# Plain stores of a gated FNet and feed-forward kernel issued by SyncE in place of GpSimd

## The chip, the cores and the metric

The kernel runs on one core of one Trainium2 chip. The metric is the device time of one launch in microseconds (us). Before the change it is 1788.1 us, the median of three runs (1788.05 to 1788.41).

## The reference, cut to what matters

```python
g = sigmoid((x * gate_w).sum(-1, keepdims=True))
a = einsum("bsd,ed->bse", x, dft_hid_re)
b = einsum("bsd,ed->bse", x, dft_hid_im)
y = einsum("ts,bse->bte", dft_seq_re, a) - einsum("ts,bse->bte", dft_seq_im, b)
h = relu(einsum("bsd,df->bsf", x, w1) + b1) ** 2
out = einsum("bsf,fd->bsd", h, w2) + b2
return g * y + (1 - g) * out
```

x is 2048 x 1024, w1 is 1024 x 3584, w2 is 3584 x 1024, the two sequence matrices are 2048 x 2048 and the two hidden ones 1024 x 1024, all in float32.

## The kernel before, in words

There are five matrix products: x (the two DFTs along the hidden dimension), a and b (the two parts of x times w1), c (the DFT along the sequence) and o (h times w2). Each is done by a scheme of Strassen and Winograd in seven products of halves, numbered 1 to 7, and most of these are split once more in the same way. So operands are sums of blocks (S1 to S4 on the left, T1 to T4 on the right). Each operand is then split in a high and a low part, rounded to the type of fast float32: ScalarE writes the high one (L203, L407), VectorE the low one (L211, L415, L418). Three matmuls (high by high, low by high, high by low) make one product of blocks. All matmuls are issued at one place (L1425). Results leave PSUM by ScalarE or VectorE (L308, L321, L329), and a group of matmuls that continues an older sum has it copied into PSUM first by ScalarE (L255).

The kernel's text holds its own planner. It first lists all operations (`Op`) and all steps of TensorE. From the fixed order of the steps it works out a due time for each operation, and then it goes backward from those to a planned start (L1134 to L1150), with SLACK (L89) held back, 3 us for SyncE and 2 us for GpSimd, and with SOON (L88), the time within which a result that is to be evicted should leave. Then it simulates the run forward. In this it has 55 slots in SBUF for blocks of 512 KB, two DMA rings (`rings`, L1182), one that SyncE and one that GpSimd feeds, which share 390 GB/s (L24, `rate`, L1185), and costs such as n/960 + 0.064 us for n elements on VectorE (L152). `try_engine` (L1326) lets each engine begin the first operation by planned start that is ready at the simulated moment, at most 15 us ahead (AHEAD, L67). GUARD (L87) holds back other work when the eviction of a PSUM group is about to be ready: within the first number of us, operations with a planned start later than the eviction's by more than the second number wait. The order in which the simulation begins operations is the order of the instructions on each engine of the chip, where semaphores alone time them. The order of the matmuls doesn't depend on the simulation.

Transfers: `load` (L164, issued at L166) and `back` (L445) are issued by SyncE. GpSimd issues three kinds. `accumulate` (L169, issued at L172) reads a block from DRAM and adds it to a block in SBUF, and `add_to` (L476) and the adding of o's part to the output (L976) are alike. Plain stores are `store` (L175, issued at L177) and `out` of the class Seven (L435, issued at L438). `store` writes what later stages read: `ab` and `h` (results of x, and of a and b), `out` (the gated part of c), `e` (sums made early, EARLY, L83) and `t` (sums that go to DRAM when made and are loaded again in a later product: THROUGH_X, THROUGH_C and THROUGH_O, L95 to L99). All `t` are blocks that an accumulating transfer has just made. `out` writes spilled results (`v`). A plain store of the gate vector of 8 KB (L901) has a line of its own. On each engine's queue instructions start in order: one that waits for a semaphore holds up those behind it.

`EARLY` gives sums that are made ahead of the stage that uses them: for b_l a store is due at 75 us and then every 15 us, four of them. The opening (`prologue`, L1438) and the last group (`by_row`, L979) have instructions of their own.

Of the kernel before, what the change touches and what calls it, by code (L numbers as in the profile page):

```python
# [16 lines left out]
P = 128  # L17
# [12 lines left out]
         5), ("a", 3), ("x", 3), ("b", 3), ("a", 7), ("x", 7), ("b", 7), ("x", 4), ("a", 4), ("b", 4), ("c", 0), ("o",  # L30
         0))
ORDER_C = (1, 2, 5, 6, 3, 7, 4)
ORDER_O = (1, 2, 5, 6, 3, 7, 4)
# [30 lines left out]
BY_DMA = {"x_l": ("S1", "S2", "S3", "S4"), "x_r": ("T1", "T4"), "h_l": ("S4",), "c_l": ("S1", "S2", "S3", "S4"),  # L64
          "c_r": ("T1", "T2", "T3", "T4"), "o_l": ("S3", "S4"), "o_r": ("T2", "T3", "T4")}
# [13 lines left out]
CHAIN = {"c": {1: 1, 2: 1, 3: 1, 4: 1, 5: 2, 6: 1, 7: 1}, "o": {3: 1, 1: 1, 2: 1, 4: 1, 6: 1, 7: 1, 5: 1}}  # L79
# [3 lines left out]
EARLY = {"a_l": (("S2", "S1"), (), 70.0, 7.5), "b_l": (("S2",), (), 75.0, 15.0), "x_r": (("T1",), (), 40.0, 7.5)}  # L83
# [3 lines left out]
GUARD = (0.7, 3.0)  # L87
SOON = {"POOL": 12.0, "ACT": 6.0, "DVE": 6.0}  # L88
SLACK = {"SP": 3.0, "POOL": 2.0, "ACT": 0.6, "DVE": 0.6}  # L89
LEAD = {"SP": 3.0, "POOL": 1.0, "ACT": 2.0, "DVE": 2.0}  # L90
GATE = (320.0, 5.0)
# [6 lines left out]
THROUGH_C = ("T2",)  # L98
THROUGH_O = ("T2",)  # L99
# [3 lines left out]
def gated_mix_kernel(ctx: ExitStack, tc: tile.TileContext, x4, xn, w4, ct, w1a, w1b, w2, b1, b2, gw, out):  # L103
# [15 lines left out]
    class Val:  # L119
# [6 lines left out]
        def ap(self):  # L126
            return self.tile[:, :, :self.width]
# [293 lines left out]

    class Seven:
# [25 lines left out]
        def keep(self, name, vs):  # L448

            far = [i for i, runs in enumerate(SPILL.get(name, ())) if self.name and self.name in runs]  # L450
            self.have[name] = vs
            there = None
            if far:
                place = self.place if name == "s" and self.name in ADD_S else None
                there = {k: self.out(v, k, place and Far(place(k).at)) for k, v in vs.items()}
            self.kept[name] = far, there, [0]

        def get(self, name):
            far, there, n = self.kept[name]
            n[0] += 1  # L460
            if n[0] - 1 in far:
                vs = {}
                for k, f in there.items():
                    vs[k] = self.back(f, k)
                    if name == "s":
                        mark = ops[-1].also = Fixed()
                        ops[-1].then = lambda t, mark=mark: setattr(mark, "ready", t)
                        self.marks.append((k, mark))
                return vs
            return self.have[name]  # L470
# [8 lines left out]
        def do(self, p):  # L479
            get, product, place = self.get, self.product, self.order.index  # L480
            first, second = (5, 7) if place(5) < place(7) else (7, 5)
            summed = self.name and self.name in SUMMED
            mid = {5: ((0, 1), 3), 7: ((1, 0), 4)}
            if p == 1:
                self.keep("one", (yield from product(1, None, None)))
            elif p == 2:
                yield from product(2, get("one"), (0, 0))
            elif p == 6:
                self.keep("u", (yield from product(6, get("one"), None)))
            elif summed and p == first:  # L490
                self.keep("s", (yield from product(p, get("u"), None)))
            elif summed and p == second:
                t = yield from product(p, None, None)
                far_s, far_u = self.name in ADD_S and self.place, self.name in ADD_U
                s, u, w = None if far_s else get("s"), self.kept["u"][1] if far_u else get("u"), {}
                assert not far_s or place(mid[first][1]) < place(second)
                for k in self.keys:
                    if far_s:
                        dst, f = self.place(k), self.kept["s"][1][k]
                        Op("POOL", 0.6, 2 * P * 4 * 512 * 2, [t[k], f] + [m for j, m in self.marks if j == k], dst,  # L500
                           lambda k=k, dst=dst: nc.gpsimd.dma_start(dst.at, t[k].ap(), accum_op=ADD)).twice = True
                    else:
                        self.final((1, 1), k, both(s[k], t[k], self.rows, k[-1]))
                    w[k] = self.add_to(t[k], k, u[k]) if far_u else both(u[k], t[k], self.rows, k[-1])
# [112 lines left out]
    def tall(name, left, right, ksteps, order, second, less, final, from_ps, by_row=None):  # L617
# [4 lines left out]
        def product(p, old, quad):  # L622
# [23 lines left out]
            l2 = {q: Inner(lambda m, j, q=q: View(base[j, q], 256 * m), INNER_L, 256) for q in range(k2)}  # L646
# [45 lines left out]
            def twice(q, p2):  # L692
                again[q].made.update({key: r2[q].of(key) for key in ("T1", "T2")})
                l_, r_ = FACTORS[p2]
                step(operand(l2[q].of(l_), p in less), operand(again[q].of(r_)), groups[p2])
# [33 lines left out]
        run = Seven(order, 4, keys, product, final)  # L729
        for p in order:  # L730
            for _ in run.do(p):
                pass

# [44 lines left out]
    def x_stage():  # L778
# [17 lines left out]
        left.update({(m, q): Side(x_block(m, q), PLUS_L, BY_DMA["x_l"],  # L796
# [3 lines left out]
        right = {(q, c): Side(lambda j, n, q=q, c=c: Far(w4[n, c, j, q], 0.0), MIX_R, BY_DMA["x_r"], through=THROUGH_W,  # L800
# [11 lines left out]
    def h_stage(part):  # L812
# [38 lines left out]
        left = {(m, q): Side(lambda i, j, m=m, q=q: Far(w1[i, m, j, q], 0.0), MIX_L, BY_DMA["h_l"], rows * P,  # L851
# [66 lines left out]
    def c_stage():  # L918
# [21 lines left out]
        left = {q: Side(lambda i, j, q=q: ab[j, q, i], PLUS_L, BY_DMA["c_l"], through=THROUGH_C,  # L940
                        made={f: c_forms[f, q] for f in C_FORMS}) for q in range(8)}
        right = {(q, c): Side(lambda j, n, q=q, c=c: Far(ct[n, c, j, q], 0.0), PLUS_R, BY_DMA["c_r"], through=THROUGH_C, made=had("c_r", (q, c)))
                 for q in range(8) for c in range(2)}
        tall("c", left, right, 8, ORDER_C, TWICE_C, LESS_C, lambda quad, k, v: end(quad, k, v, lambda: v.tile),
# [11 lines left out]
    def o_stage():  # L956
# [37 lines left out]

        left = {q: Side(lambda i, j, q=q: Far(w2[i, j, q], 0.0), MIX_L, BY_DMA["o_l"], through=THROUGH_O, made=had("o_l", q)) for q in range(7)}
        right = {(q, c): Side(lambda j, n, q=q, c=c: h_far[j, q, 2 * n + c], PLUS_R, BY_DMA["o_r"], through=THROUGH_O,
                             made={f: o_forms[f, q, c] for f in O_FORMS})
                 for q in range(7) for c in range(2)}
        tall("o", left, right, 7, ORDER_O, TWICE_O, LESS_O, lambda quad, k, v: end(quad, k, v, lambda: v.tile),
# [36 lines left out]
    def had(side, at):  # L1036
        return {f: early[side, at, f] for f in EARLY.get(side, ((),))[0]}

# [3 lines left out]
    runs = {"x": x_stage(), "a": h_stage(0), "b": h_stage(1)}  # L1042
    for name, p in ORDER:
        a, b = len(ops), len(steps)
        if name in ("c", "o"):
            (c_stage if name == "c" else o_stage)()
        else:
            parts = [runs[r].do(ALIKE[p] if r == "x" and TOGETHER else p) for r in name]
            while parts:
                parts = [g for g in parts if next(g, done) is not done]  # L1050
        marks.append((f"{name}{p}", a, len(ops), b, len(steps)))
# [507 lines left out]
```

## Time and profile before

| what | us |
|---|---|
| median of three runs | 1788.1 |
| the profiled execution | 1788.53 |
| its span, from the first to the last instruction | 1786.7 |
| TensorE busy | 1780.1 |
| VectorE busy | 1637.1 |
| ScalarE busy | 1027.1 |
| GpSimd busy | 296.6 |

The profiled execution is 1.83 us longer than its span and 0.43 us longer than the median. Busy time doesn't count the issuing of DMAs on SyncE. On GpSimd the issuing instruction itself is shown as busy.

### The profile page before, as it was taken

How to read it: one execution, taken by the hardware profiler on the slowest of the kernel's cores; microseconds unless marked ns; L12 is line 12 of the kernel's file. 1: busy time of each engine (PE TensorE's matmuls, PEld its weight loads, DVE VectorE, ACT ScalarE, POOL GpSimd, SP SyncE). 2: the span in 40 equal slices, each digit the busy share in tenths (PEclk: the TensorE clock that was granted, in tenths of full speed). 3: DMA queues.
4: the chain of work that ended last, by engine and by line, in shares of the span. 5: the costliest groups of instructions: out<-in, count | busy, mean ns of one | idle time of the engine just before them, and what ended most of it. 6: DMA issues, size and time to landing. Idle time of an engine off the chain costs nothing.

```text
span 1786.7 us, 21834 instructions
## 1 busy us (share of the span) xinstructions
PE 1780.1 (100%) x7868; PEld 1473.8 (82%) x7868; DVE 1637.1 (92%) x1696; ACT 1027.1 (57%) x1224; POOL 296.6 (17%) x422
## 2 busy tenths in 40 slices
PE   9999999999999999999999999999999999999998
PEld 8888888888888888888888888888888888888887
DVE  8886999999799897999998999659999998999998
ACT  7444744324669576876574737436576434673753
POOL 0102211011211322101133202212000022211120
PEclk9999999999999999999999999999999999999999
DMA  9919989988969999789899959999675996997993
GB/s 378 387 56 291 286 296 309 362 323 265 291 249 370 311 283 334 259 291 308 234 241 269 240 175 318 303 274 268 233 258 191 375 274 184 313 315 169 299 269 73
DMA packets 144237, 488.03 MB, mean 273 GB/s; under 512 B 15728, under 2 KB 29376, under 8 KB 144128
## 3 DMA queue, kind: packets, MB, share of 16 engines
q0 software_dynamic: 58928, 210.27, 45.8%
q1 hardware_dynamic: 84496, 275.17, 42.0%
q8 instruction: 62, 1.02, 0.2%
q10 hardware_dynamic: 704, 1.18, 0.2%
q14 instruction: 47, 0.39, 0.1%
HBM read 376.98 MB, written 109.58 MB: 272 GB/s over the span
## 4 chain that ended last, share of the span: by engine, by line
PE 99%; ACT 1%; DMA 0%; DVE 0%; issue 0%
PE ps L1425 99%; DMA raw<-in_x 0%; ACT hi L203 0%; ACT ps L255 0%; DVE o L960 0%; DVE o L989 0%; ACT both L407 0%; ACT acc L308 0%; ACT hi L1464 0%; ACT both L203 0%
## 5 line engine op out<-in xcount | busy, mean ns | idle before, releaser
L1425 PE MATMUL ps<-hi,both 128*128 128x512 f32 x2072 | 640.8, 389 | 0.3 <-ACT ps L255 0.3
L1425 PE MATMUL ps<-hi 128*128 128x512 f32 x1574 | 611.3, 389 | 0.5 <-ACT hi L1464 0.5
L1425 PE MATMUL ps<-lo,hi 128*128 128x512 f32 x1574 | 611.2, 389 | 0.0
L1425 PE MATMUL ps<-hi,lo 128*128 128x512 f32 x1574 | 611.2, 389 | 0.0
L1425 PEld LDWEIGHTS ps<-hi,both 128*128 128x128 f32 x2072 | 389.1, 188 | 82.0 <-ACT ps L255 1.4
L203 ACT ACTIVATE hi<-raw 128x1024 fp32r<-128x1024 f32 (+1 forms) x315 | 321.7, 1037 | 217.0 <-DVE raw L182 82.9
L1425 PE MATMUL ps<-lo,both 128*128 128x512 f32 x1036 | 403.3, 389 | 0.0
L211 DVE TENSOR_TENSOR lo<-raw,hi 128x1024 fp32r<-128x1024 f32 (+1 forms) x279 | 337.0, 1218 | 43.6 <-ACT hi L203 39.0
L1425 PEld LDWEIGHTS ps<-hi 128*128 128x128 f32 x1574 | 295.5, 188 | 62.0 <-ACT hi L1464 0.8
L1425 PEld LDWEIGHTS ps<-lo,hi 128*128 128x128 f32 x1574 | 295.5, 188 | 61.3
L1425 PEld LDWEIGHTS ps<-hi,lo 128*128 128x128 f32 x1574 | 295.6, 188 | 61.2
L203 ACT ACTIVATE hi<-sum 128x1024 fp32r<-128x1024 f32 (+1 forms) x230 | 234.5, 1030 | 182.3 <-DVE sum L182 123.5
L211 DVE TENSOR_TENSOR lo<-sum,hi 128x1024 fp32r<-128x1024 f32 (+1 forms) x195 | 235.2, 1211 | 6.2 <-ACT hi L203 3.7
L1425 PEld LDWEIGHTS ps<-lo,both 128*128 128x128 f32 x1036 | 194.5, 188 | 40.2
L308 ACT ACTIVATE acc<-ps 128x1024 f32<-128x1024 f32 (+1 forms) x142 | 139.5, 987 | 123.9 <-PE ps L1425 118.8
L321 DVE TENSOR_TENSOR acc<-acc,ps 128x1024 f32<-128x1024 f32 (+1 forms) x152 | 172.5, 1140 | 39.9 <-PE ps L1425 38.1
L182 DVE TENSOR_TENSOR raw<-raw 128x1024 f32<-128x1024 f32 (+1 forms) x131 | 152.0, 1178 | 0.1
L203 ACT ACTIVATE both<-sum 128x512 fp32r<-128x512 f32 x148 | 92.2, 625 | 101.3 <-DVE sum L388 57.3
L255 ACT ACTIVATE ps<-acc 128x1024 f32<-128x1024 f32 (+1 forms) x83 | 81.2, 980 | 69.4 <-DVE acc L321 54.1
L321 DVE TENSOR_TENSOR back<-back,ps 128x1024 f32<-128x1024 f32 x64 | 71.9, 1129 | 14.8 <-PE ps L1425 14.3
L407 ACT ACTIVATE both<-raw 128x512 fp32r<-128x512 f32 x111 | 68.4, 619 | 27.6 <-PE ps L1425 16.7
L182 DVE TENSOR_TENSOR sum<-raw,sum 128x1024 f32<-128x1024 f32 (+1 forms) x65 | 77.8, 1197 | 1.0 <-PE ps L1425 0.9
(69 smaller groups left out, 1193.3 us busy)
## 6 DMA issues: line engine op xcount, KB each, us to landing
raw<-h SPq DMA_DIRECT2D x92, 512.0 KB, 6.5
raw<-in_ct SPq DMA_DIRECT2D x91, 512.0 KB, 7.6
raw<-in_w SPq DMA_DIRECT2D x81, 512.0 KB, 7.5
back<-v SPq DMA_DIRECT2D x48, 512.0 KB, 6.5
raw<-in_ct POOLq DMA_DIRECT2D x48, 512.0 KB, 12.7
raw<-ab SPq DMA_DIRECT2D x40, 512.0 KB, 13.7
t<-raw POOLq DMA_DIRECT2D x38, 512.0 KB, 12.4
sum<-t SPq DMA_DIRECT2D x38, 512.0 KB, 18.3
```

The lines of the kernel that those rows point to most:

```text
L182: Op("DVE", c, l, [a, b], w, lambda: nc.vector.tensor_tensor(w.ap(), a.ap(), b.ap(), op=op), over=[a, b])
L203: nc.scalar.activation(self.hi()[:, k, :], src(v)[:, k, :], AF.Copy, scale=-1.0 if less else 1.0)
L211: nc.vector.tensor_tensor(a, b, c, op=SUB)
L255: lambda rp=rp, k=k, e=e, v=v: nc.scalar.activation(self.ps[rp][:, :k, :], v.tile[:, e:e + k, :], AF.Copy),
L308: group.take(seg, rp, Op("ACT", c, l, [], w, lambda: nc.scalar.activation(view(w.tile, rows, rp), view(group.ps[rp], rows, rp), AF.Copy, s ...
L321: nc.vector.tensor_tensor(a, b, d, op=ADD)
L407: Op("ACT", c, l, [v.base], hi, lambda: nc.scalar.activation(self.hi(), cols(v), AF.Copy, scale=-1.0 if less else 1.0), then=lambda t: set ...
L1425: nc.tensor.matmul(group.ps[r // group.per][:, r % group.per, :], a()[:, kk, r * P:(r + 1) * P], b()[:, kk, :], start=first and kk + n == ...
```

## The change

All calls of `store` and of `out` are issued by SyncE, at a planned cost of 0.06 us in place of 0.6, and the planner counts them to SyncE's ring. GpSimd keeps the accumulating transfers and the store of the gate vector at L901. Five numbers of the planner change (EARLY for b_l, GUARD, SOON for GpSimd, which now also serves SyncE, GATE by 0.8 us, CHAIN for product 7 of c), and in stage o the sum S1 of left block 0 goes through DRAM. The remaining edits restate tables or add paths that this setting doesn't take: BY_DMA and THROUGH_C as counts of blocks (8 is all of them), c and o in the same list of the order as the rest and in the same order as before, and `Lefts`, which with MERGE empty makes the operands that `Inner` made. CHAIN for product 7 of c isn't used, as that product isn't split again.

```diff
-ORDER_C = (1, 2, 5, 6, 3, 7, 4)
-ORDER_O = (1, 2, 5, 6, 3, 7, 4)
...
-CHAIN = {"c": {1: 1, 2: 1, 3: 1, 4: 1, 5: 2, 6: 1, 7: 1}, "o": {3: 1, 1: 1, 2: 1, 4: 1, 6: 1, 7: 1, 5: 1}}
+CHAIN = {"c": {1: 1, 2: 1, 3: 1, 4: 1, 5: 2, 6: 1, 7: 2}, "o": {3: 1, 1: 1, 2: 1, 4: 1, 6: 1, 7: 1, 5: 1}}
...
-EARLY = {"a_l": (("S2", "S1"), (), 70.0, 7.5), "b_l": (("S2",), (), 75.0, 15.0), "x_r": (("T1",), (), 40.0, 7.5)}
+EARLY = {"a_l": (("S2", "S1"), (), 70.0, 7.5), "b_l": (("S2",), (), 68.7, 11.9), "x_r": (("T1",), (), 40.0, 7.5)}
+MERGE = ""
+STORES = "SP"
...
-GUARD = (0.7, 3.0)
-SOON = {"POOL": 12.0, "ACT": 6.0, "DVE": 6.0}
+GUARD = (1.2, 8.0)
+SOON = {"POOL": 18.0, "ACT": 6.0, "DVE": 6.0}
...
-GATE = (320.0, 5.0)
+GATE = (320.8, 5.0)
...
-THROUGH_C = ("T2",)
-THROUGH_O = ("T2",)
+THROUGH_C = {"T2": 8}
+THROUGH_O = {"T2": 8, "S1": 1}
...
     def store(dst, v, ap=None):
-        Op("POOL", 0.6, 2 * P * 4 * v.width * 2 / 2, [v], dst,
-           lambda: nc.gpsimd.dma_start(dst.at, v.ap() if ap is None else ap(v.tile)))
+        q, c = (nc.sync, 0.06) if STORES == "SP" else (nc.gpsimd, 0.6)
+        Op(STORES, c, 2 * P * 4 * v.width * 2 / 2, [v], dst,
+           lambda: q.dma_start(dst.at, v.ap() if ap is None else ap(v.tile))).soon = True
...
+        def of(self, key):
...
+            return operand(self.plain.of(key), self.less)
...
         def out(self, v, k, f=None):
 
             f, n = f or far(f"v{len(ops)}"), min(2, self.rows - 2 * k[-1])
-            Op("POOL", 0.6, P * 4 * 512 * n, [v], f, lambda: nc.gpsimd.dma_start(f.at[:, :n, :], v.tile[:, :n, :]))
+            q, c = (nc.sync, 0.06) if STORES == "SP" else (nc.gpsimd, 0.6)
+            Op(STORES, c, P * 4 * 512 * n, [v], f, lambda: q.dma_start(f.at[:, :n, :], v.tile[:, :n, :])).soon = True
             return f
...
-                step(operand(l2[q].of(l_), p in less), operand(r2[q].of(r_)), groups[p2])
+                step(l2[q].of(l_), operand(r2[q].of(r_)), groups[p2])
...
-            o.due = min(o.due, (made or at[o.step]) + SOON[o.eng])
+            o.due = min(o.due, (made or at[o.step]) + SOON.get(o.eng, SOON["POOL"]))
```

## Rows read from the trace of the kernel before

**Rows 1.** The page: span, busy time and share of each engine.

```profile
span 1786.7 us, 21834 instructions
...
PE 1780.1 (100%) x7868; PEld 1473.8 (82%) x7868; DVE 1637.1 (92%) x1696; ACT 1027.1 (57%) x1224; POOL 296.6 (17%) x422
```

**Rows 2.** The chain that ended last, in order of time: start, length, what.

```profile
5.79 1669.49 PE ps L1425 x7362
...
1682.64 1.02 ACT ps L255
...
1683.70 96.91 PE ps L1425 x426
...
1782.81 0.69 DVE o L989
```

**Rows 3.** Waits of TensorE's weight loads: us in total, times, longest.

```profile
PEld ps L1425 <- ACT ps L255: 1.4, 3, 0.7
```

**Rows 4.** Timeline of TensorE's matmuls: start, us, engine, line, operation.

```profile
1660.37 0.39 PE L1425 MATMUL ps<-lo,both 128*128 128x512 f32 x1
...
1678.73 0.39 PE L1425 MATMUL ps<-lo,both 128*128 128x512 f32 x1
...
1781.57 0.39 PE L1425 MATMUL ps<-hi,both 128*128 128x512 f32 x1
```

**Rows 5.** Plain stores on GpSimd, L177: ns min/median/max, first and last start.

```profile
L177 POOL DMA_DIRECT2D t<-raw x38: 532/552/1519, 152.3 to 1531.4; - x38
...
L177 POOL DMA_DIRECT2D h<-h x12: 532/534/563, 177.5 to 740.8; - x12
```

**Rows 6.** The same of the spills, L438.

```profile
L438 POOL DMA_DIRECT2D v<-acc x28: 532/534/580, 236.8 to 421.1; - x28
L438 POOL DMA_DIRECT2D v<-back x12: 532/545/563, 375.1 to 426.5; - x12
```

**Rows 7.** The loads at L166 on SyncE: semaphore waits, issues, landing.

```profile
L166 SPq EVENT_SEMAPHORE  x441: 17/17/31748, 23.4 to 1728.0; - x147
...
L166 SPq DMA_DIRECT2D raw<-in_ct x91: 327/328/630, 670.4 to 1134.8; - x91
...
DMA to landing us min/median/max: 3.1/8.2/30.4
```

**Rows 8.** What SyncE's queue waited for: us in total, times, longest.

```profile
SPq L166 <- PE ps L1425: 560.9, 163, 20.3
...
SPq L166 <- DMA raw<-in_ct: 123.7, 19, 58.7
```

**Rows 9.** What GpSimd's and ScalarE's queues waited for, two rows of the list.

```profile
POOL out L177 <- DVE acc L930: 76.1, 8, 48.3
...
ACT hi L203 <- DMA sum<-in_ct: 6.6, 1, 6.6
```

**Rows 10.** VectorE's costliest group: busy us, mean ns, idle before and its releasers.

```profile
L211 DVE TENSOR_TENSOR lo<-raw,hi 128x1024 fp32r<-128x1024 f32 (+1 forms) x279 | 337.0, 1218 | 43.6 <-ACT hi L203 39.0 <-PE ps L1425 3.9 <-DMA h<-acc 0.6
```

**Rows 11.** The accumulating transfers, L172: issues, who waited for them, landing.

```profile
L172 POOL DMA_DIRECT2D raw<-in_ct x48: 835/860/1882, 801.9 to 1166.2; - x48
...
  POOL t L177: 25.0, 11
...
DMA to landing us min/median/max: 5.5/11.3/27.3
```

**Rows 12.** DMA queues: packets, MB, share of 16 engines (q0 is GpSimd's, q1 SyncE's).

```profile
q0 software_dynamic: 58928, 210.27, 45.8%
q1 hardware_dynamic: 84496, 275.17, 42.0%
```

**Rows 13.** Windows of 45 us: busy of PE, PEld, DVE, ACT, POOL; clock; DMA; GB/s.

```profile
45.00:90.00 45.00, 45.00 (x200) 37.30 (x199) 39.49 (x39) 22.27 (x25) 5.28 (x9) 1.00 1.01 384
90.00:135.00 45.00, 45.00 (x200) 37.26 (x199) 37.75 (x33) 22.18 (x24) 1.78 (x3) 1.00 0.18 58
...
810.00:855.00 45.00, 45.00 (x200) 37.30 (x199) 45.00 (x53) 30.55 (x38) 6.84 (x9) 1.00 1.05 307
...
1485.00:1530.00 45.00, 45.00 (x200) 37.30 (x199) 40.75 (x48) 26.90 (x34) 6.76 (x10) 1.00 0.66 176
```

**Rows 14.** Timeline of GpSimd: last early sum; first and last of four stores.

```profile
92.09 0.69 POOL L177 DMA_DIRECT2D e<-raw  x1 [12.54 <-DVE raw L182]
...
888.90 0.57 POOL L177 DMA_DIRECT2D out<-acc  x1 [15.44 <-DVE acc L932]
...
898.45 0.56 POOL L177 DMA_DIRECT2D out<-acc  x1 [2.04 <-DVE acc L932]
```

**Rows 15.** Timeline of SyncE from 895 to 1000 us: its only row.

```profile
989.45 6.68 SPq L166 DMA_DIRECT2D raw<-in_ct  x2
```

More of the change, by code (lines that the diff above doesn't have):

```diff
@@ L420, in __init__, with once, sums, mix @@
             Op("DVE", c, l, [v.base, mid], self.done, low)
+    class Lefts:
+        def __init__(self, a, b, less, fresh):
+            self.a, self.b, self.less, self.made = a, b, less, {}
+            self.mixed = fresh and "m" in MERGE
+            self.plain = Inner(lambda m, j: View((a, b)[j], 256 * m), INNER_L, 256)
+        def once(self, key, make):
+            if key not in self.made:
+                self.made[key] = make()
+            return self.made[key]
+        def sums(self):
+            a, b, w, w2 = self.a, self.b, Val("sum"), Val("sum")
+            c, l = dve(512)
+            Op("DVE", c, l, [a, b], w, lambda: nc.vector.tensor_tensor(
+                w.tile[:, :, :256], a.tile[:, :, 256:], b.tile[:, :, 256:], op=ADD))
+            Op("DVE", c, l, [w, a], w2, lambda: nc.vector.tensor_tensor(
+                w2.tile[:, :, 256:], w2.tile[:, :, :256], a.tile[:, :, :256], op=SUB), over=[w], must=True)
+            return w2
+        def mix(self):
+            if "s" in MERGE:
+                self.once("sums", self.sums)
+            else:
+                self.plain.of("S2")
+            a, w = self.a, Val("sum")
+            c, l = dve(512)
+            Op("DVE", c, l, [a], w, lambda: nc.vector.tensor_tensor(
+                w.tile[:, :, 256:], w.tile[:, :, :256], w.tile[:, :, 256:], op=SUB), over=[a], must=True)
+            return w
+        def of(self, key):
+            if key in ("S1", "S2") and "s" in MERGE:
+                w = self.once("sums", self.sums)
+                return Half(self.once("S12", lambda: Operand(w, self.less)), 256 * (key == "S2"))
+            if key in ((0, 0), "S3") and self.mixed:
+                w = self.once("mix", self.mix)
+                return Half(self.once("AS", lambda: Operand(w, self.less)), 256 * (key == "S3"))
+            if key in ((0, 1), (1, 1)) and "a" in MERGE:
+                return Half(self.once("AA", lambda: Operand(self.b, self.less)), 256 * key[0])
+            if key == "S4" and "s" in MERGE:
+                v, w, b = Val("sum", 256), self.once("sums", self.sums), self.b
+                c, l = dve(512)
+                Op("DVE", c, l, [b, w], v, lambda: nc.vector.tensor_tensor(
+                    v.ap(), b.tile[:, :, :256], w.tile[:, :, 256:], op=SUB))
+                return operand(v, self.less)
+            return operand(self.plain.of(key), self.less)
@@ L448, in keep @@
         def keep(self, name, vs):
-            far = [i for i, runs in enumerate(SPILL.get(name, ())) if self.name and self.name in runs]
+            far = [{k for k in vs if self.name in runs or self.name.upper() in runs and k[0]}
+                   for runs in SPILL.get(name, ())]
             self.have[name] = vs
             there = None
-            if far:
+            if any(far):
                 place = self.place if name == "s" and self.name in ADD_S else None
-                there = {k: self.out(v, k, place and Far(place(k).at)) for k, v in vs.items()}
+                there = {k: self.out(v, k, place and Far(place(k).at)) for k, v in vs.items() if any(k in f for f in far)}
             self.kept[name] = far, there, [0]
@@ L460, in get @@
             n[0] += 1
[L461 to L470, printed above, removed]
+            keys = far[n[0] - 1] if n[0] <= len(far) else ()
+            vs = dict(self.have[name])
+            for k in sorted(keys):
+                vs[k] = self.back(there[k], k)
+                if name == "s":
+                    mark = ops[-1].also = Fixed()
+                    ops[-1].then = lambda t, mark=mark: setattr(mark, "ready", t)
+                    self.marks.append((k, mark))
+            return vs
         def add_to(self, v, k, f):
@@ L483, in do @@
             mid = {5: ((0, 1), 3), 7: ((1, 0), 4)}
-            if p == 1:
+            apart = place(second) < place(6)
+            if apart and p in (first, second):
+                self.keep("vt"[p == second], (yield from product(p, None, None)))
+            elif apart and p in (3, 4):
+                mine, other = "vt" if (p == 3) == (first == 5) else "tv"
+                old = self.sum(get("u"), get(mine))
+                yield from product(p, old, mid[5 if p == 3 else 7][0])
+                if place(p) < place(7 - p):
+                    v = get(other)
+                    for k in self.keys:
+                        self.final((1, 1), k, both(old[k], v[k], self.rows, k[-1]))
+            elif p == 1:
                 self.keep("one", (yield from product(1, None, None)))
@@ L645, in product @@
             base = {(j, q): left[2 * q + j].of(l) for j in range(2) for q in range(k2)}
-            l2 = {q: Inner(lambda m, j, q=q: View(base[j, q], 256 * m), INNER_L, 256) for q in range(k2)}
+            l2 = {q: Lefts(base[0, q], base[1, q], p in less, l not in ("S1", "S2")) for q in range(k2)}
             raw = {}
@@ L694, in twice @@
                 l_, r_ = FACTORS[p2]
-                step(operand(l2[q].of(l_), p in less), operand(again[q].of(r_)), groups[p2])
+                step(l2[q].of(l_), operand(again[q].of(r_)), groups[p2])
             def once():
@@ L727, in product, with by_dma @@
             return new
[L729 to L732, printed above, removed]
+        return Seven(order, 4, keys, product, final, name)
+    def by_dma(side, n):
+        return [f for f, k in BY_DMA[side].items() if (n + 1) * k // 8 > n * k // 8]
     class Part(Far):
@@ L1041, in gated_mix_kernel @@
     sums_early()
-    runs = {"x": x_stage(), "a": h_stage(0), "b": h_stage(1)}
+    runs = {"x": x_stage(), "a": h_stage(0), "b": h_stage(1), "c": c_stage(), "o": o_stage()}
     for name, p in ORDER:
         a, b = len(ops), len(steps)
[L1045 to L1050, printed above, removed]
+        parts = [runs[r].do(ALIKE[p] if r == "x" and TOGETHER else p) for r in name]
+        while parts:
+            parts = [g for g in parts if next(g, done) is not done]
         marks.append((f"{name}{p}", a, len(ops), b, len(steps)))
```

38 lines of the change are left out of this document (22 added, 16 removed).

## The prediction

> **What bounds the kernel now.** The page comes first: TensorE is busy for 1780.1 of the 1786.7 us, VectorE for 92%, GpSimd for 17% [rows 1]. A busy TensorE need not be a fast one, so the chain that ended last is next. It runs through matmuls from 5.79 us to the end, leaves them once, at 1682.6 us for ScalarE's copy into PSUM at L255, and ends with VectorE's two additions for the last output [rows 2]. The list of waits says how much time TensorE lost: 1.4 us before three weight loads, all behind L255 [rows 3]. No wait of TensorE on a DMA stands in it.
>
> The timeline checks this. In an undisturbed stretch 27 times three matmuls take from 1660.37 to 1678.73 us, so one takes 18.36 / 81 = 0.2267 us [rows 4]. The page counts 7868 matmuls, of which 38 warm the engine up (WARM), so 7830 work. From the first start at 5.79 us [rows 2] to the last at 1781.57 [rows 4] lie 7829 intervals, at that pitch 1774.6 us; 1775.8 were taken. The lost 1.2 us are the three waits. The granted clock is 1.00 of full speed, 2.4 GHz, in the windows shown [rows 13].
>
> So the time is 5.8 us of opening, 1774.6 us of matmuls at an even pitch, some 1.2 to 1.4 us of waits, and 5.1 us from the last matmul's start to the end of the span, with 1.8 us outside it: 1788.5 us, 0.4 above the median. The change takes no matmul away, adds none, and leaves opening and last group as they are. **Only the waits can change**: downward by 1.4 us, upward without such a limit.
>
> **The change, part by part.** *Stores leave GpSimd.* Eight kinds at L177, 38 of `t` down to 12 of `h`, make 166, and L438 has 28 and 12, so 206 issues of about 0.55 us, 113 us of GpSimd's time [rows 5, 6]. Nothing on the chain waits for GpSimd, which is busy for 17%: 0 us. What the accumulating transfers gain is that they no longer stand behind a store that waits for its data; a store of c's output held this queue for up to 48.3 us [rows 9]. These transfers can start sooner, but TensorE never waited for one: again 0, at best a share of the 1.4 us.
>
> *Stores join SyncE.* With the sum S1 of stage o there are 207. At the 0.33 us of a load's issue [rows 7] they occupy SyncE for 68 us of 1787. A load behind one starts 0.33 us later. What covers that is the lead of the operands: ScalarE once waited 6.6 us for an accumulated block, and TensorE didn't notice [rows 9]. Taken: 0.
>
> *The new waits on SyncE.* A store waits there for its data, and the loads behind it wait too; those who wait for the loads are ScalarE's and VectorE's splits and the accumulating transfers, which add to a loaded block. The planner begins a store in its simulation only when the data is ready, so the chip's wait is how far the chip runs behind the plan. For stores of VectorE's results there is a term for this: the plan has 1024 / 960 + 0.064 = 1.131 us for an operation of 1024 elements, and the commonest one has a mean of 1.218 us, with the shorter form in it [rows 10]. That is at least 0.087 us each, and in a stretch of 45 us with 53 operations and no idle time [rows 13] at most 53 x 0.087 = 4.6 us. For the 38 `t`, which wait for an accumulating transfer, it is the landing: median 11.3 us, longest 27.3 us, so up to 16.0 us late [rows 11]. Against that, SyncE's queue waits now, too, and more: 560.9 us in all for matmuls that free a slot, up to 58.7 us at one load for an accumulated block, and 31.7 us in one semaphore wait [rows 7, 8], and TensorE waited for none of these. Bounds: -1.4 us, if earlier accumulating transfers remove the old waits, and 16.0 - 6.6 = +9.4 us, if one such landing finds only the smallest cover that I can show. Nearer to 0, since 4.6 us is inside the cover of 6.6 us, and the longest present waits cost nothing: I take 0.
>
> *Bytes.* GpSimd's queue carried 210.3 MB at 45.8% of the engines' time, SyncE's 275.2 MB at 42.0% [rows 12]. The stores are 206 blocks of 512 KB or less, so at most 108 MB of the first. They move to the other ring, and the sum stays. In 45 to 90 us, where GpSimd issues stores and no accumulating transfer, the two queues move 384 GB/s at a share of 1.01 [rows 13], about what the planner assumes for either, so I see no dearer or cheaper byte. But the share is also 1.05 in 810 to 855 us [rows 13], where both queues are full. There a ring that holds loads and stores puts each store ahead of a load: four stores of c's output, from 888.9 to 898.5 us [rows 14], are 2.1 MB; if the rings share evenly, as the planner has it, that takes 10.9 us at half of 384 GB/s, and less the cover of 6.6 us it is 4.3 us. I take 0, as SyncE issues no load between these stores and 989 us [rows 15].
>
> The Trainium skill (DMA: Bandwidth & Descriptors, SWDGE vs HWDGE vs iDMA) says that the two kinds of issuer feed different queues inside each DMA engine, and that the engine takes turns between them. By that rule the loads would share their turn with the stores, while the accumulating transfers had theirs alone, and the sum would be up by an estimated 4 us. No row of the kernel before shows turns being taken.
>
> *S1 of stage o.* One store and one load more, 1.05 MB, 2.7 us at 384 GB/s. The DMA engines stand at 0.66 in one window of that stage, 1485 to 1530 us [rows 13], 15 us of room. 0, at most 2.7 us if it falls where there is none. A slot is free for the length of a product in return.
>
> *The early sums of b_l.* Their dates move ahead by 6.3, 9.4, 12.5 and 15.6 us, in a stretch with the engines full to 90 us and at 0.18 after it [rows 13]. The last early store left at 92.09 us [rows 14]; its three loads of 384 KB and the store, 1.6 MB or 4.1 us, may now fall before 90 us, ahead of loads that are needed. Below the cover of 6.6 us: 0; at most 4.1 us.
>
> *GUARD, SOON, GATE.* They reorder VectorE and ScalarE. All three old waits are behind L255, whose place in ScalarE's order GUARD touches, so this could remove them or make as many again: from -1.4 to +1.4 us, taken as 0.
>
> **Sum**: 1788.53 + 0 for the profiled execution, 1788.1 for the median.
>
> **Rivals.** *SyncE's queue is held* (slower). A `t` store waits for a late accumulating transfer, the loads behind it land too late, and TensorE waits on a split. For it: in the kernel before, stores of `t` already waited 25.0 us in all for these transfers [rows 11], and the store now has every later load behind it. Against it: the long waits on SyncE that cost nothing. It bites from a hold of 6.6 us and can be told apart from no change from 10.2. One at 16.0 us costs 9.4: 1797.5 us.
>
> *The shared ring delays loads* (slower): one burst of four stores at 4.3 us, 1792.4 us. It decides where loads are urgent behind the burst; for it speaks the share of 1.05, against it rows 15. This is also what the skill's page would bring about.
>
> *The waits at L255 vanish*: 1788.1 - 1.4 = 1786.7 us. GpSimd's freed queue and the new GUARD speak for it, but those waits hang on ScalarE, which doesn't wait for a DMA there.
>
> *The change does less than it says.* One plain store, of 8 KB, stays on GpSimd (L901), and the planner may begin each store at the moment at which GpSimd would have. That is 1788.1 again and is part of the forecast.
>
> *A gain of over 0.2%* needs 3.6 us, more than all waits; opening or end would have to shrink, and nothing edits them.
>
> **How the numbers follow.** No change, within a wait or two: 0.69. Waits gone: 0.15. SyncE held: 0.10. Shared ring: 0.04. A larger gain: 0.02. About 0.2%, 3.6 us, is what a measurement can tell from no change; the first two cases are inside it: 0.84, with 0.14 slower and 0.02 faster. The lower end is the case without waits less the spread of the three runs: 1786.7 - 0.3 = 1786.4. The upper end leaves out the two slower cases and allows six more waits of the present mean, 1.4 / 3 = 0.47 us: 1788.1 + 2.8 = 1790.9 us.
>
> **What would show it.** Right: 7868 matmuls at 0.2267 us, no wait of TensorE on a DMA or on a split of a loaded block, and GpSimd left with 422 - 206 = 216 instructions [rows 1]. The held queue would show as a long wait of SyncE before a store of `t`, followed by a wait of ScalarE on a load, and one of TensorE on ScalarE. The shared ring would show as landing times of loads above the present median of 8.2 us [rows 7] beside bursts of stores. A matmul pitch other than 0.2267 us, or an opening or end of another length, would make the whole reasoning wrong.

## The result and the profile after

The change makes the kernel slower by 0.27%: 1793.1 us (median of 9 runs, 1791.91 to 1795.32) against 1788.1 us (9 runs, 1787.99 to 1788.44), ratio 1.0027, 95% interval 1.0019 to 1.0036. The forecast was no change, 1788.1 us, and its range ended at 1790.9. The profiled execution took 1793.79 us. Its page (busy time, share, instructions; then the queues, q0 GpSimd's and q1 SyncE's):

```profile
span 1792.0 us, 21793 instructions
...
PE 1782.4 (99%) x7868; PEld 1474.5 (82%) x7868; DVE 1634.6 (91%) x1696; ACT 1027.7 (57%) x1224; POOL 185.6 (10%) x216
...
q1 hardware_dynamic: 114960, 377.42, 56.1%
q0 software_dynamic: 30928, 109.07, 31.4%
```

Beside [rows 1, 12]: GpSimd has the 216 instructions that were foreseen, 101 MB have gone from q0 to q1, and the two shares add up to 87.5% where they were 87.8%. As many matmuls are done, and the span is 5.3 us longer. Where these are lost is in the list of what TensorE's weight loads waited for (us in total, times, longest), and in their timeline (start, length, in brackets the wait ahead of it):

```profile
PEld ps L1493 <- DVE lo L214: 4.3, 3, 2.2
...
PEld ps L1493 <- ACT ps L258: 0.9, 2, 0.6
```

```profile
184.48 0.19 PEld L1493 LDWEIGHTS ps<-hi,lo 128*128 128x128 f32 x1 [1.66 <-DVE lo L214]
192.03 0.19 PEld L1493 LDWEIGHTS ps<-hi,lo 128*128 128x128 f32 x1 [2.19 <-DVE lo L214]
```

The waits sum to 5.2 us where they were 1.4 [rows 3]: 3.8 us more. They aren't spread: 3.85 us lie in two, at 184 and 192 us, both for a low part that VectorE makes. The rest comes right behind the second. First two windows of 5 us (the columns of [rows 13]), then matmuls from TensorE's timeline:

```profile
190.00:195.00 5.00, 3.23 (x12) 2.37 (x11) 5.00 (x5) 0.68 (x1) 0.00 (x0) 0.85 1.06 275
195.00:200.00 5.00, 5.00 (x20) 4.02 (x19) 2.60 (x3) 1.24 (x2) 0.00 (x0) 0.81 1.02 391
```

```profile
193.57 0.63 PE L1493 MATMUL ps<-hi,lo 128*128 128x512 f32 x1
194.00 0.63 PE L1493 MATMUL ps<-hi 128*128 128x512 f32 x1
...
196.56 0.54 PE L1493 MATMUL ps<-hi 128*128 128x512 f32 x1
196.94 0.40 PE L1493 MATMUL ps<-lo,hi 128*128 128x512 f32 x1
```

The granted clock has a mean of 0.85 and 0.81 here. From 193.57 to 196.94 us eight intervals take 3.37 us, 0.42 us each in place of 0.2267 [rows 4]: about the lower of the two levels, 1.2 GHz. That costs 3.37 - 8 x 0.2267 = 1.6 us. So 3.8 + 1.6 = 5.4 us of the span's 5.3, and the opening is 0.1 us shorter. The nine runs bear this out: the three with a mean clock of 1.000 took 1791.9 to 1792.1 us, which is 3.8 above the kernel before, the waits alone; the profiled one has 0.999.

The second wait is on the chain that ended last (start, length, what):

```profile
178.33 11.86 DMA h<-acc
...
190.76 1.23 DVE lo L214
...
192.03 469.78 PE ps L1493 x2064
...
1688.82 96.91 PE ps L1493 x426
```

The last row shows that nothing else has changed: the last 426 matmuls took 96.91 us before, too [rows 2]. For the low part, though, the timeline of VectorE shows something that the chain doesn't:

```profile
185.48 1.21 DVE L324 TENSOR_TENSOR acc<-acc,ps 128x1024 f32<-128x1024 f32 x1
189.62 1.22 DVE L324 TENSOR_TENSOR acc<-acc,ps 128x1024 f32<-128x1024 f32 x1 [2.92 <-PE ps L1493]
190.76 1.22 DVE L214 TENSOR_TENSOR lo<-sum,hi 128x1024 fp32r<-128x1024 f32 x1
```

VectorE stands idle for 2.92 us before an eviction that has to wait for TensorE's matmuls, and the split for the next product is behind it in VectorE's order. The chain names a store of h, which landed at 190.19 us; the order alone would have kept the split to 190.76. So there are two suspects: transfers (stores on SyncE, and what they delay), and the planned order.

### The profile page after: what moved, and what is told of

It is laid out like the page before. It is cut to its first block, busy times and chain, and to the rows that moved or that the text cites. A ratio compares the mean times of both kernels' runs of the same rounds, so it can differ in the third digit from the quotient of the medians.

```text
span 1792.0 us, 21793 instructions
## 1 busy us (share of the span) xinstructions
PE 1782.4 (99%) x7868; PEld 1474.5 (82%) x7868; DVE 1634.6 (91%) x1696; ACT 1027.7 (57%) x1224; POOL 185.6 (10%) x216
## 3 DMA queue, kind: packets, MB, share of 16 engines
q1 hardware_dynamic: 114960, 377.42, 56.1%
q0 software_dynamic: 30928, 109.07, 31.4%
## 4 chain that ended last, share of the span: by engine, by line
PE 97%; DMA 1%; DVE 1%; ACT 1%; issue 0%; DVEq 0%; ACTq 0%
PE ps L1493 97%; DMA h<-acc 1%; DMA raw<-in_w1a 0%; DVE lo L214 0%; DMA raw<-in_x 0%; ACT acc L907 0%; DVE acc L332 0%; ACT ps L258 0%; ACT hi L206 0%; DVE both L421 0%; DVE o L1030 0%; DVE sum L185 0%; DVE o L1059 0%; DVE sum L391 0%; DVE both L214 0%
## 5 line engine op out<-in xcount | busy, mean ns | idle before, releaser
L206 ACT ACTIVATE hi<-raw 128x1024 fp32r<-128x1024 f32 (+1 forms) x309 | 314.8, 1036 | 202.7 <-DVE raw L185 93.9
L206 ACT ACTIVATE hi<-sum 128x1024 fp32r<-128x1024 f32 (+1 forms) x236 | 240.7, 1031 | 197.1 <-DVE sum L185 144.6
L214 DVE TENSOR_TENSOR lo<-raw,hi 128x1024 fp32r<-128x1024 f32 (+1 forms) x272 | 324.4, 1202 | 31.0 <-ACT hi L206 27.2
L214 DVE TENSOR_TENSOR lo<-sum,hi 128x1024 fp32r<-128x1024 f32 (+1 forms) x202 | 241.8, 1200 | 12.9 <-ACT hi L206 4.7
L185 DVE TENSOR_TENSOR raw<-raw 128x1024 f32<-128x1024 f32 (+1 forms) x126 | 144.9, 1165 | 1.9 <-DMA raw<-in_w1a 1.7
L185 DVE TENSOR_TENSOR sum<-raw,sum 128x1024 f32<-128x1024 f32 (+1 forms) x69 | 81.9, 1186 | 3.4 <-DMA raw<-in_w1a 2.4
```

What stands on the lines that cost most here:

```text
L185: Op("DVE", c, l, [a, b], w, lambda: nc.vector.tensor_tensor(w.ap(), a.ap(), b.ap(), op=op), over=[a, b])
L206: nc.scalar.activation(self.hi()[:, k, :], src(v)[:, k, :], AF.Copy, scale=-1.0 if less else 1.0)
L214: nc.vector.tensor_tensor(a, b, c, op=SUB)
```

## The experiments

Some leave the order of the kernel after (or before) as planned and change only which engine issues a store; others let the planner make a new order. Times are medians of ten runs, or of four for the kernels at 1800 us and above; the kernel before, measured beside them, took 1788.1 to 1788.3 us.

**The order of the kernel after, its stores given back to GpSimd.** Three kernels: the 39 `t` stores, the 64 of `h`, or all 207. The planner still counts them to SyncE's ring.

```diff
-    def store(dst, v, ap=None):
+    def store(dst, v, ap=None, by=None):
...
+        q = by or q
...
-                store(f, v)
+                store(f, v, by=nc.gpsimd)
```

> The changed kernel with its plan and its orders kept, but the 39 stores of t issued by GpSimd at the place that they had in the plan. Held queue (a store of t waits 7.3 us on SyncE for its accumulating transfer and holds the loads of w1 behind it): the load of w1 that started at 165.1 us starts near 158, TensorE's two waits at 184.5 and 192.0 us are gone, and the time is 1788 to 1789 us. Shared ring (stores of h take 11.9 us to land behind loads, so slots come free late): the waits stay, 1792 to 1795 us. Plan (the other numbers placed the sums of x late): the waits stay, 1792 to 1795 us.

> The changed kernel with its plan kept, but the 64 stores of h issued by GpSimd. Held queue: the store of t at 164.7 us still holds the loads, so the waits near 184 and 192 us stay, 1792 to 1795 us. Shared ring: the stores of h land in about 7 us again, the wait at 192 us goes, and the time is 1788 to 1790 us. Plan: 1792 to 1795 us.

> The changed kernel with its plan kept, but all 207 plain stores issued by GpSimd, each at its planned place among the accumulating transfers. Held queue and shared ring both: 1788 to 1789 us, no wait at 184 and 192 us. Plan: the order that the new numbers gave is the cause whoever issues, so 1791 us or more, with waits near 184 and 192 us.

Measured: 1792.4 us (ratio 1.0024, 1.0014 to 1.0033), 1793.2 (1.0025, 1.0016 to 1.0035) and 1792.0 (1.0022, 1.0013 to 1.0031). The two waits stay in all three. In the second the chain shows why it can't be the store of h that holds the split back:

```profile
159.96 22.45 PE ps L1494 x99
...
182.44 0.25 DVE acc L325
...
183.04 1.23 DVE lo L215
...
184.32 5.09 PE ps L1494 x21
189.40 0.02 issue
189.43 0.25 DVE acc L325
...
190.56 1.23 DVE lo L215
191.79 0.04 issue
191.84 3.24 PE ps L1494 x13
```

No transfer is in it, at either wait: matmuls, the eviction that needed them, the split, matmuls. TensorE waits for 1.59 and again for 2.19 us. What follows: with this order the loss is there whichever engine issues the stores; between all on GpSimd and all on SyncE lie 1.1 us, which the intervals don't tell from nothing. Why the planner put the split there (whether its simulation had a slot for it earlier) isn't settled by this.

**A new order: the planner's two settings.** SOON 12 in place of 18, STORES "POOL" in place of "SP" (planned and issued), or both, all other numbers as after. The last kernel is the one before with stores planned and issued on SyncE, and its old numbers.

```diff
-STORES = "SP"
+STORES = "POOL"
...
-SOON = {"POOL": 18.0, "ACT": 6.0, "DVE": 6.0}
+SOON = {"POOL": 12.0, "ACT": 6.0, "DVE": 6.0}
```

> The changed kernel with SOON at 12 us in place of 18. If the number SOON moved the sums of x late and made the waits: one of the two waits at 184 and 192 us is gone and the other is shorter, 1789 to 1790.5 us. If the issuing engine on the chip makes them: both stay, 1792 us or more. If only the ring in the plan makes them: both stay.

> The changed kernel with the stores planned and issued on GpSimd, all other new numbers kept (SOON 18). If SOON alone is enough for waits: a wait of over 1 us between 180 and 195 us remains, 1789 to 1791 us. If it takes the stores on SyncE (plan or chip): no wait there, 1788 us.

> The changed kernel with the stores planned and issued on GpSimd and SOON at 12 us; GUARD, EARLY, GATE and S1 of stage o stay new. If the two together (the ring in the plan and SOON) are the whole cause: no wait between 150 and 200 us and, with the new GUARD, fewer waits behind the copies into PSUM than before: 1787 to 1788 us, below both kernels. If GUARD, EARLY or S1 have a part in the loss: 1789 us or more.

> The kernel before with the stores planned and issued on SyncE and nothing else changed: SOON stays at 12 us, GUARD, EARLY, GATE and S1 of stage o as before. Held queue: a store of t still stands before loads of w1, so TensorE waits between 150 and 200 us, 1790 us or more. Plan: the issuing engine isn't the cause, 1788 to 1789 us. Shared ring: 1790 us or more, with stores of h that land in over 10 us.

| stores planned and issued by | SOON 12 | SOON 18 |
|---|---|---|
| GpSimd | 1787.0 us (0.9994, 0.9984 to 1.0004) | 1789.4 (1.0008, 0.9998 to 1.0017) |
| SyncE | 1791.5 (1.0021, 1.0011 to 1.0030) | 1793.1 (the kernel after) |
| SyncE, numbers of before | 1791.5 (1.0017, 1.0008 to 1.0027) | |

So the change splits up: the other new numbers take off 1.1 us (1788.1 to 1787.0), the stores on SyncE put on 4.5, and SOON 18 another 1.6. The parts depend on the order in which they are taken: on GpSimd SOON 18 costs 2.4, after which SyncE costs 3.7, and with the numbers of before SyncE costs 3.2 (1788.3 beside it). The 1.1 and the 1.6 lie within the intervals.

One pair tells the plan from the issuing. The kernel with all stores given back to GpSimd (1792.0 us) has the plan of SyncE; the one at 1789.4 has the same numbers and the same issuer, but a plan for GpSimd. So the plan alone costs 2.5 us, and no run of the one (1791.59 to 1793.52) is as fast as any of the other (1789.30 to 1789.99).

On SyncE with SOON 12 the waits of TensorE's working weight loads, behind the opening, sum to 4.6 us:

```profile
PEld ps L1493 <- DVE lo L214: 3.2, 4, 1.1
...
PEld ps L1493 <- DVE lo L212: 0.8, 1, 0.8
PEld ps L1493 <- ACT acc L311: 0.6, 1, 0.6
```

With GpSimd and 12, the list of waits has one row for a working weight load, in the opening:

```profile
PEld ps L1493 <- ACT hi L1532: 0.6, 1, 0.6
```

Its span is 1785.5 us, and this is the version below both kernels. All its runs (1786.87 to 1787.71) are below the lowest of the runs of before beside it, 1787.96, though the interval of the ratio takes in 1.

**The old order, all stores issued by SyncE.** Planner and orders of the kernel before; only the issuing engine differs. And the same to the best order above.

```diff
-           lambda: nc.gpsimd.dma_start(dst.at, v.ap() if ap is None else ap(v.tile)))
+           lambda: nc.sync.dma_start(dst.at, v.ap() if ap is None else ap(v.tile)))
```

> The kernel before with its plan and with the orders of TensorE, VectorE and ScalarE kept, but all 206 plain stores issued by SyncE, each at the place that it had in the plan. Plan (the orders that came from planning the stores on SyncE's ring cost the time, not the issuing): 1788 to 1789 us, no wait between 150 and 200 us. Held queue or shared ring on the chip: 1791 us or more, with waits of TensorE there.

> The kernel with the new numbers, planned for GpSimd and with SOON 12, which had no wait and took 1787.0 us, issued by SyncE at the planned places. If issuing by SyncE in an order made for GpSimd costs what it did in the kernel before (12.6 us): 1798 to 1801 us, with a wait near 674 us. If that was an accident of the old numbers: 1787 to 1790 us.

1800.7 us (1.0070, 1.0055 to 1.0085) and 1800.3 (1.0068, 1.0053 to 1.0083): 12.6 and 13.3 us above their partners. In the first, the weight loads' timeline has a wait near 674 us and the chain a load that takes 22 us:

```profile
674.26 0.29 PEld L1425 LDWEIGHTS ps<-hi 128*128 128x128 f32 x1 [6.08 <-ACT hi L203]
```

```profile
649.80 22.32 DMA raw<-in_w1a
```

In the timeline of the matmuls, 15 intervals from 668.22 to 681.90 us take 13.7 us in place of 3.4: 10.3 of the 12.6 us, waits and lower clock together. What else moves between 640 and 672 us is told by the view of DMA for that window (queues: packets, MB, share; issues: KB, median us to landing), first of the kernel before, then of this one:

```profile
q0 software_dynamic: 1877, 6.72, 66.0%
q1 hardware_dynamic: 1025, 2.77, 25.0%
...
raw<-in_w1a SPq DMA_DIRECT2D x4, 512.0 KB, 9.6
...
acc<-v POOLq DMA_DIRECT2D x2, 512.0 KB, 10.7
```

```profile
q0 software_dynamic: 1456, 4.26, 68.0%
q1 hardware_dynamic: 1512, 4.46, 38.2%
...
acc<-v POOLq DMA_DIRECT2D x3, 512.0 KB, 21.0
...
raw<-in_w1a SPq DMA_DIRECT2D x3, 512.0 KB, 22.3
acc<-v POOLq DMA_DIRECT2D x4, 256.0 KB, 20.0
```

Two accumulating transfers start in this window of the kernel before, seven in this one. Before, six more stood behind stores of `ab` that waited for evictions, and went at 674.72 us, as GpSimd's timeline of the kernel before has it:

```profile
674.72 5.30 POOL L476 DMA_DIRECT2D acc<-v  x6
```

Without the stores nothing holds them, and the queues' shares go from 91% to 106%. Fewer bytes were moved in that window (8.7 MB for 9.5), by busier engines. This is a new suspect: accumulating transfers that no longer stand behind stores crowd out the loads.

**The old order, some stores by SyncE.** The same for `h`; `h` by ScalarE; `t`; all but `h` and `t`; `h` and `ab`. The last one's edit:

```diff
-    def store(dst, v, ap=None):
+    def store(dst, v, ap=None, by=nc.gpsimd):
...
-           lambda: nc.gpsimd.dma_start(dst.at, v.ap() if ap is None else ap(v.tile)))
+           lambda: by.dma_start(dst.at, v.ap() if ap is None else ap(v.tile)))
...
-            store(ab[n, q, k[1]], v)
+            store(ab[n, q, k[1]], v, by=nc.sync)
...
-            store(Part(dst, at, tiles), w2_, lambda t: t[:, :tiles, :])
+            store(Part(dst, at, tiles), w2_, lambda t: t[:, :tiles, :], nc.sync)
```

> The kernel before with its plan and its orders kept, the 64 stores of h alone issued by SyncE. In the run with all stores on SyncE, TensorE waited 6.1 us at 674 us for loads of w1 that stood behind eight stores of h and landed after 22 us, and 1.4 us at 184 us. Shared ring (stores of h ahead of loads): the wait at 674 us comes back with at least half its length, 1793 to 1798 us. Held queue (stores of t that wait for accumulating transfers): no such wait, 1788 to 1789 us. Freed accumulating transfers (GpSimd runs ahead once the stores have left it): part of the wait, 1790 to 1796 us.

> The same with the 64 stores of h issued by ScalarE, which makes h: they leave GpSimd's queue and don't stand ahead of loads on SyncE's. Shared ring: no long wait at 674 us, 1788 to 1790 us (ScalarE spends some 0.35 us on each issue). Freed accumulating transfers: the loads of w1 land late all the same, 1791 us or more, with a wait near 665 to 675 us. Held queue: 1788 to 1790 us.

> The same with the 38 stores of t alone issued by SyncE. Held queue: SyncE waits for accumulating transfers to land, up to 17 us as in the run with all stores, and TensorE waits somewhere, 1790 us or more. Shared ring: few stores lie ahead of loads, 1788 to 1789 us.

> The same with the stores of ab, out, e and v (104 of them) issued by SyncE, h and t on GpSimd. Shared ring: the six stores of ab between 658 and 676 us stand ahead of later loads of w1 and ct, a wait of 1 to 3 us near 665 to 680 us, 1789 to 1792 us. Held queue: VectorE's results come late for the plan by less than 5 us, within the cover of 6.6 us, 1788 to 1789 us.

> The kernel before with its plan kept, stores of h and of ab (96) issued by SyncE, the others by GpSimd. Freed accumulating transfers: these are the stores that stood between the accumulating transfers at 640 to 675 us, so the wait at 674 us comes back, 1794 us or more. Shared ring with a sum of single shares: 0.7 + 0.1 us, 1788 to 1790 us.

| stores moved | us | ratio, interval |
|---|---|---|
| `h` | 1789.0 | 1.0007, 0.9997 to 1.0016 |
| `h`, to ScalarE | 1791.6 | 1.0018, 1.0008 to 1.0027 |
| `t` | 1788.4 | 1.0001, 0.9992 to 1.0010 |
| all but `h` and `t` | 1788.3 | 1.0000, 0.9991 to 1.0010 |
| `h` and `ab` | 1801.5 | 1.0081, 1.0063 to 1.0099 |

The cost isn't a sum over stores: `h` alone and `ab` alone (in "all but `h` and `t`") cost next to nothing, both together 13.3 us. The stretch before 674 us says why. With only `h` moved (the profiled run is the slowest of its ten, 1791.8 us), the first loads of w1a leave later (651.41 us; 645.11 before), behind eight stores of h on SyncE, but the six accumulating transfers still stand behind stores of ab and go at 678.03, and the loads land in 8.6 us. With ab moved and h kept, the six go at 648.86 us, behind stores of h, but three loads have left from 645.38 on, ahead of them, and the four land in 11.6. With both moved, the accumulating transfers go from 638.41 us on, the loads follow at 650.49, and land in 21.7. Moving `t` costs nothing, so SyncE's waits for them don't reach TensorE. The run on ScalarE is inconclusive: the six go at 675.71 us there, what it costs may be ScalarE's time for the issues, and its profiled run, the fastest of the ten at 1789.0 us, doesn't show the cost.

**Holding the accumulating transfers back without the stores.** All stores by SyncE as above, and at the place of each GpSimd copies a 128x1 piece of the block, whose result nothing uses; then the same for `h` and `ab` alone.

```diff
+    def hold(v):
+        nc.gpsimd.tensor_copy(held_back[:, 0:1], v.tile[:, 0, 0:1])
...
-           lambda: nc.gpsimd.dma_start(dst.at, v.ap() if ap is None else ap(v.tile)))
+           lambda: (nc.sync.dma_start(dst.at, v.ap() if ap is None else ap(v.tile)), hold(v)))
```

> The kernel before with its plan and its orders kept, all plain stores issued by SyncE, and in each store's old place on GpSimd a copy of one column of the stored block (128 elements), which waits for the same data: the accumulating transfers stay as held back as they were. Freed accumulating transfers (with every store gone, GpSimd runs ahead and its accumulating transfers crowd out the loads at 640 to 675 us): the wait at 674 us is gone, 1788 to 1791 us. Shared ring or held queue on SyncE: the wait stays, 1797 us or more, since SyncE's queue is the same as in the run that gave 1800.7 us.

> The plan and the compute orders of the kernel before; the stores of h and ab (96 of 206) are issued by SyncE, as in e16_h_and_ab_by_sync (1801.5 us, TensorE waiting 5.7 us near 674 us, loads of w1a landing in 21 to 24 us), and at the place where GpSimd had issued each of them it now makes a copy of a 128x1 piece of the stored block, whose result nothing uses, so that GpSimd's accumulating transfers wait again for the same events as before. If it is the accumulating transfers, freed from behind the stores, that crowd the loads: the long wait near 674 us is gone, the loads of w1a there land in 8 to 14 us, and the time is 1788 to 1793 us, the extra over 1788 being what the copies themselves cost on GpSimd. If it is that the stores stand on SyncE's ring or hold SyncE's queue: the wait near 674 us stays, the loads land in 20 us or more, and the time stays at 1799 us or above. A time above 1799 without that wait would mean that the copies delay something else, and the total says nothing.

The first took 1809.2 us (1.0129, 1.0105 to 1.0153). Its wait at 674 us is gone, but the copies take 1.0 to 1.7 us in the mean for most tiles, there are 206 of them, and ScalarE waited 13.4 us for two of them; TensorE waits elsewhere, so the total says nothing. The second took 1791.7 us (1789.91 to 1793.50; 1.0018, 1.0008 to 1.0028), 9.9 us less than without the copies. Its DMA view from 640 to 672 us and the whole of its waits for VectorE's low parts:

```profile
q1 hardware_dynamic: 2726, 8.60, 68.5%
q0 software_dynamic: 440, 1.57, 25.0%
...
raw<-in_w1a SPq DMA_DIRECT2D x3, 512.0 KB, 10.6
...
acc<-v POOLq DMA_DIRECT2D x2, 512.0 KB, 8.8
```

```profile
PEld ps L1429 <- DVE lo L215: 2.3, 1, 2.3
```

The stores are still on SyncE's queue and ring, more bytes than before are on it, and the loads leave even later, at 652.19 us. Yet they land in 10.6 us, since only two accumulating transfers start in that window. So for a fixed order the cost near 674 us is that of accumulating transfers that run ahead of the loads; a late start behind stores on SyncE lets them get ahead, and does no harm there without them.

It isn't free everywhere. Of the 3.5 us that are left over the kernel before, 2.3 are a wait at 201 us, which the kernel without copies has, too (2.1 us), and so has the profiled run with `h` alone moved (2.3). The chain leads from it to a load right behind a store of h on SyncE (start, length, what):

```profile
182.70 0.34 SPq L181
...
183.15 14.53 DMA raw<-in_w1a
```

The same load left at 182.71 us in the kernel before and landed in 9.1 us. This is what the rival of the shared ring foresaw, on a small scale; what else may slow the load there wasn't tried.

**A plan that doesn't know.** The kernel after with SOON 12, issued by SyncE, but with the planner counting stores to GpSimd's ring.

```diff
-            rings[o.eng].append([n, o.lat / n / DMA_RATE, o])
+            rings["POOL" if o.st else o.eng].append([n, o.lat / n / DMA_RATE, o])
```

> The changed kernel with SOON 12 (1791.5 us) whose planner counts the stores to GpSimd's ring, while SyncE issues them. Ring in the plan (stores and loads in one ring make the plan late at 184 us): the wait at 184 us goes, 1788.5 to 1790 us. Ring on the chip: the wait at 184 us stays or a longer one comes, 1791 us or more.

1801.2 us (1.0072, 1.0057 to 1.0087), against 1791.5 with stores counted to SyncE's ring. TensorE's longest wait is 3.1 us at 671.65 us, and the chain has the late load again:

```profile
649.43 20.09 DMA raw<-in_w1a
```

With the stores counted to SyncE's ring no load is on the chain from 640 to 680 us. So here the order comes out much better when the ring in the plan is the one on the chip.

## Why the prediction was wrong

**The step that failed** is the term for GUARD, SOON, GATE, "from -1.4 to +1.4 us, taken as 0", and with it the lack of any term for a new order. The edit makes the planner order everything anew, with stores on another ring, and the prediction priced that by the old waits at L255 alone. The runs showed evictions and splits in another sequence: 3.8 us of waits for splits that stand behind an eviction, and 1.6 us of lower clock in the profiled run. The waits stay with all stores given back to GpSimd (1792.0 us), so it is the order and not the issuing that costs. Of the 5.0 us, planning and issuing on SyncE is 4.5 and SOON 1.6, and the other numbers gave 1.1 back; where only the plan differs, it is 2.5 us. Why the planner orders it so at 184 and 192 us stays open: whether the freed transfers, which the plan simulates, are the reason wasn't tried apart. A changed plan has no bound in the waits of the old one, as the prediction itself said ("upward without such a limit") and then didn't use.

**A second step** was wrong, though it isn't where the kernel after lost its time: "These transfers can start sooner, but TensorE never waited for one: again 0, at best a share of the 1.4 us." It took earlier accumulating transfers for a gain or nothing. TensorE doesn't wait for them, but for loads that they slow down. In the old order all stores on SyncE cost 12.6 us; with `h` and `ab` alone it is 13.3, and 9.9 of these come back when the transfers are held. The new order spares most of that (with the old numbers 1791.5 in place of 1800.7). The price was to be had from [rows 12]: q1's 42.0% for 275.2 MB are 0.153% per MB; at that, the stores' 108 MB take 16.5 of q0's 45.8%, and 29.3% are left for 102 MB, nearly twice as much per byte. The planner has it, too: it counts an accumulating transfer's bytes twice (L169 to L172). "I see no dearer or cheaper byte" was read in a window without accumulating transfers. The bytes term itself was right: the shares' sum hasn't changed.

**The rivals.** SyncE's queue held by `t`: not borne out (1788.4 us when they alone move; 1792.4 when they alone go back). In the old order SyncE is held by stores of `h`, which alone costs 0.7 us. The shared ring: not as stated, since near 674 us the same bytes on it do no harm while the accumulating transfers are held; at 201 us it fits a wait of 2.3 us in the old order. Both had the right sign, but neither is what the kernel after loses by, as its waits stay with all stores on GpSimd. The waits at L255 didn't vanish in the kernel after (0.9 us left), but did in the one with GpSimd and SOON 12, and at 1787.0 us it came near that rival's 1786.7.

**What held**: as many matmuls at the same pitch, 96.91 us for the last 426; SyncE's own issue time (68 us) shows no cost, as 38 of the stores, and 104 others, moved for 0.2 us or less; GpSimd's freed 111 us show no gain; opening and end keep their length to 0.2 us. Of the signs to look for, waits of TensorE on a split did come. The one for the shared ring didn't: loads land in 3.2/8.1/30.4 us (shortest, median, longest), as before [rows 7], and the kernel is slower all the same. The Trainium skill (DMA: Bandwidth & Descriptors, SWDGE vs HWDGE vs iDMA) gives plain transfers to SyncE or ScalarE and accumulating ones to GpSimd, by what a transfer does. The runs here differ: plain stores on SyncE are 4.5 us dearer with a plan made for it, 12.6 without.

## What to carry to other kernels

A queue that holds a transfer up can be what keeps the transfers in time with each other. Before stores leave a queue, look at which transfers stand behind them, what these cost the DMA engines, and which urgent loads they would meet; a wait in an engine that isn't the bottleneck isn't free to remove. Where a planner makes the order, test the issuing engine in a fixed order apart from the new order.

## What the runs showed of the hardware

An accumulating transfer takes nearly twice the engines' time of a plain one per byte. After the change q0 has nothing else but 8 KB: 31.4% for 109.07 MB are 0.288% per MB, and q1's 56.1% for 377.42 MB are 0.149%, a factor of 1.94. The Trainium skill (DMA: Bandwidth & Descriptors, Rules for kernel authors) says that such a transfer reads its destination and writes it later. The factor agrees with two passes, which no run here shows by themselves.

In the profiled run of after, waits of 1.66 and 2.19 us were followed by eight matmul intervals at the lower clock level; three of the nine runs show none of it in their mean clock. The kernel with all stores given back to GpSimd has the same two waits (1.66 and 2.19 us), and in its profiled run the granted clock is 1.00 behind them (columns of [rows 13]):

```profile
190.00:195.00 5.00, 3.23 (x15) 2.64 (x15) 5.00 (x5) 0.49 (x1) 0.00 (x0) 1.00 1.05 265
195.00:200.00 5.00, 5.00 (x24) 4.14 (x23) 3.88 (x5) 2.01 (x2) 1.09 (x2) 1.00 1.03 333
```

In the old order on SyncE the wait of 6.1 us had windows of 0.66, 0.50 and 0.82 from 670 to 685 us behind it. So two short waits cost 1.6 us more than they last, or nothing more.

A GpSimd copy of one element per partition, which was to be a cheap stand-in for a wait, took 1.7 us in the mean on 88 blocks that VectorE or ScalarE makes:

```profile
L177 POOL COPY held_back<-acc 128x1 f32<-128x1 f32 x88 | 152.3, 1731 | 324.5 <-DVE acc L325 96.9 <-ACT acc L842 84.6 <-DVE acc L934 68.5
```

The mean is made by a few long ones: the shortest of the 88 took 0.18 us, the median 0.78 and the longest 24.2 (spans on this engine are rough).
